# Where the one-hot rows of the mask come from: one load on ScalarE's queue and a copy on GpSimd, with clears and the identity moved between engines

## The chip, the cores and the metric

The kernel runs on one core of one Trainium2 chip. Its time is the device time of one execution in microseconds (us). A profiled execution gives, besides, a span from the first to the last instruction and the trace that is quoted below. The engines are TensorE (PE, its weight loads PEld), VectorE (DVE), ScalarE (ACT), GpSimd (POOL) and SyncE (SP); SPq, ACTq and POOLq are transfers issued from the queues of those engines.

## The reference

Block-sparse attention over 4 batches, 8 heads, 768 positions and 64 channels, and behind it a mixer over the positions and a two-layer network:

```python
# attention, block = 32, 24 blocks
scores = scale * (q @ k^T)
mask = |blk_i - blk_j| <= 1, or the first or last block on either side,
       or kb in sampled_blocks[qb]           # 3 sampled blocks per block of queries
attn = softmax(where(mask, scores, -1e9))
x = (attn @ v), heads side by side           # (4, 768, 512)
# mixer and network
u = x + (x^T @ U @ V)^T                      # U: 768x32, V: 32x768
out = u + max(u @ w_ch1, 0) @ w_ch2          # 512 -> 2048 -> 512
```

The inputs are float32 (`sampled_blocks` integers), the output is float32.

## The kernel before

Work goes by 16 pairs of heads, 4 for each batch. The head dimension of one head is 64, so a head's q or k, turned, fills 64 partitions. The four pairs of the first batch carry the mask in the score product itself: the other 64 partitions of the same tile hold, for q, the **one-hot rows** (24 rows by 768 columns, row z is 1 where the column's query lies in block z) and, for k, the **mask rows** (24 rows that hold 0 or -240 for each block of queries against each key). One product of 128 rows then gives score plus mask. The tiles are `qres[0]`, `qres[1]`, `kres[0]` and `kres[1]`, parts of one tile `res` of 128 x 4 x 2 x 768 halves. Head 0 has its data in partitions 0 to 63 and its mask rows from partition 64 on; head 1 has its data in 64 to 127 and its mask rows from partition 0 on (`mrows`). What lies beside the 24 rows must be zero. From batch 1 on, scores are plain and are multiplied by a 0/1 `mask` tile, which is made from the product of `kmask` (the mask rows, zero elsewhere) and the one-hot rows (`mask_part`, lines 944 to 955).

The opening block (lines 234 to 349) is written out by hand and each engine runs its instructions in the order written:

- Each queue's transfers. SP loads q and k of head 0, the one-hot rows of head 1 and then of head 0 (`one_hot`, line 187), q and k of head 1, then v of pair 0 and all of pair 1, `moe_U`, the second set (`second_set`: one-hot rows into `qres[1]`, mask rows copied from `kres[0]` into `kres[1]` and `kmask`), `moe_V`. ScalarE's queue loads `small` (identity in halves, block numbers, fixed mask) and `sb` (the sampled blocks).
- VectorE clears the mask halves of `qres[0]` and `kres[0]`, `bias` and `Ut`, and then makes `bias` (24 x 48, the mask by blocks) out of `sb` in three instructions (lines 311, 315, 318).
- ScalarE loads its table with a first exponential and makes `id32`, the identity in float32, out of `small` (line 307).
- TensorE runs seven products on a constant (`keep_warm`), turns head 0's q and k in float32 with `id32` (`first_turn`, line 226), and spreads `bias` over the columns with `mask_half` (line 279), whose operand is head 1's one-hot rows. `first_row` (line 297) and `mask_row` (line 287) bring the results out of PSUM into `qres[0]` and `kres[0]`.
- GpSimd clears `qres[1]` and `kres[1]`, sets the ones columns of `vt`, casts head 1's q and k (line 213), clears `Vt` and `kmask` (line 343), and then casts what each load brings (line 131).

Behind it a long `PLAN` string gives the order of everything else, a word for each step. Its first words are scores of head 0 (`S0 S3 e e S5 B0`: `S` one score block, line 987; `B` two, line 1006; `e` its exponential on ScalarE, lines 996 and 1014), then head 1's turns (`Z`, line 359), value products (`A`, line 421), the turns of pair 1 (`R`, line 960) and the mask products (`K`, line 946). Later stages are the other batches' scores (line 1037), the first layer (line 692) and the second (line 767).

Of the kernel before, what the change touches and what calls it, by code (L numbers as in the profile page):

```python
# [12 lines left out]
FP32 = mybir.dt.float32  # L13
# [6 lines left out]
P = 128  # L20
# [3 lines left out]
def kernel(  # L24
# [14 lines left out]
    nc = tc.nc  # L39

    B, H, S, D = q.shape
    BLK = 32
    NB = S // BLK
# [13 lines left out]
    ii = np.arange(NB)  # L57
# [6 lines left out]
    ).astype(np.float32)  # L64
    cols = np.arange(S)
    blk = ((cols % P) * T + cols // P) // BLK
    ohT_np = (blk[None, :] == ii[:, None]).astype(np.float16)
    small_np = np.zeros((P, NB + 1 + P // 2), np.float32)
    small_np[:NB, :NB] = (ms_np - 1.0) * -MASK_BIAS
    small_np[:NB, NB] = ii  # L70
# [3 lines left out]
    ohT_dr = nc.inline_tensor(ohT_np, name="one_hot_const")  # L74
# [14 lines left out]
    def bank(n, shape, dtype):  # L89
        ap = PS[:, n, :]  # L90
        if dtype != FP32:
            ap = ap.bitcast(dtype)
        ap = ap[:, 0 : int(np.prod(shape[1:]))]
        return ap.rearrange("p (a b) -> p a b", a=shape[1]) if len(shape) > 2 else ap
# [3 lines left out]
    def psc2():  # L98
        ring["psc"] += 1
        return PS[:, (0, 3)[ring["psc"] % 2] :][:, 0:2]  # L100
# [4 lines left out]
    id16 = small[:, NB + 1 :].bitcast(FP16)  # L105
# [5 lines left out]
    kmask = consts.tile([P, S], FP16, name="kmask")  # L111
    res = consts.tile([P, 4, 2, S], FP16, name="res")
    qres = [res[:, i] for i in range(2)]
    kres = [res[:, 2 + i] for i in range(2)]
    drows = [slice(0, D), slice(D, P)]
    mrows = [slice(D, D + NB), slice(0, NB)]
# [5 lines left out]
    Ut = wpool.tile([P, T, P], FP16)  # L122
    Vt = wpool.tile([P, T, P], FP16)
# [52 lines left out]
    def first_load(h, n, queue):  # L176

        src, nm = ((q, "qld"), (k, "kld"))[n]
        if h == 0:
            lds[nm] = ldpool.tile([P, 2, T, D], FP32, tag="ld" + nm, name=nm)  # L180
            sts[0, nm] = stpool.tile([P, T, 2, D], FP16, tag="st" + nm, name="st" + nm)
        queue.dma_start(
            out=lds[nm][:, h], in_=src[0, h].rearrange("(p t) d -> p t d", t=T)
        )

    def one_hot(i, h):
        nc.sync.dma_start(out=qres[i][mrows[h], h, :], in_=ohT_dr.ap())

    warm = nc.const_aps.tensor(1.0, [P, 512], mybir.dt.bfloat16)
    bias = consts.tile([P, 2, D], FP16)  # L190

    def second_set():
        for h in range(2):
            one_hot(1, h)
            nc.sync.dma_start(out=kres[1][mrows[h], h, :], in_=kres[0][mrows[h], h, :])
        nc.sync.dma_start(out=kmask[mrows[0], :], in_=kres[0][mrows[0], 0, :])

    def load_mix_u():
        uld = ldpool.tile([P, T, R], FP32, tag="ldu", name="uld", bufs=1)
        nc.sync.dma_start(out=uld, in_=moe_U.rearrange("(p t) r -> p t r", t=T))  # L200
        nc.gpsimd.tensor_copy(out=Ut[:, :, 0:R], in_=uld)
# [9 lines left out]
    def first_cast(h, n, copy):  # L211
        nm = ("qld", "kld")[n]
        copy(out=sts[0, nm][:, :, h], in_=lds[nm][:, h])
# [3 lines left out]
    id32 = consts.tile([P, P], FP32)  # L217

    def first_turn(n, c):

        nm = ("qld", "kld")[n]
        twos = ((0, 1, 2), ()) if n == 0 else ((0,), (1, 2))
        pt = pw[:, 1, 0:HS] if n == 0 else bank(5 + c, [P, HS], FP32)
        first_out[n, c] = pt
        for j, t in enumerate(twos[c]):
            nc.tensor.matmul(
                pt[:, j * P : (j + 1) * P],
                lds[nm][:, 0, 2 * t : 2 * t + 2].rearrange("p t d -> p (t d)"),
                id32,
                is_transpose=True,  # L230
                start=(j == 0), stop=(j == len(twos[c]) - 1), skip_group_check=True,
            )

    with tc.manual_schedule(
        engines={
            mybir.EngineType.PE,
            mybir.EngineType.DVE,
            mybir.EngineType.Activation,
            mybir.EngineType.SP,
            mybir.EngineType.Pool,  # L240
        }
    ):
        first_load(0, 0, nc.sync)
        first_load(0, 1, nc.sync)
        nc.scalar.dma_start(out=small, in_=small_dr.ap())
        nc.scalar.dma_start(
            out=sb[0:NB].rearrange("k z r w -> k (z r w)"),
            in_=sampled_blocks.bitcast(I32)
            .rearrange("z r -> (z r)")[None, :]
            .broadcast_to([NB, NB * 6]),  # L250
        )
        for h in (1, 0):
            nc.vector.memset(qres[0][(slice(D, P), slice(0, D))[h], h, :], 0.0)
            one_hot(0, h)
        nc.vector.memset(bias, 0.0)
        for h in range(2):
            nc.vector.memset(kres[0][(slice(D, P), slice(0, D))[h], h, :], 0.0)
        for n in range(2):
            first_load(1, n, nc.sync)
        for tile_ in (qres[1], kres[1]):  # L260
            nc.gpsimd.memset(tile_.bitcast(FP32), 0.0)
        for vt in vts:
            nc.gpsimd.memset(vt[:, :, :, D : D + 1], 1.0)
        first = consts.tile([P, 1], FP32)
        nc.scalar.activation(
            out=first, in_=nc.const_aps.tensor(1.0, [P, 1], FP32), func=AF.Exp
        )
        pw = psc2()

        def keep_warm(n, cols=512):  # L270
            for _ in range(n):
                nc.tensor.matmul(
                    pw[:, 0, 0:cols], warm[:, 0:P], warm[:, 0:cols], start=True, stop=True
                )

        pks = [bank(2, [P, HS], FP32), bank(7, [P, HS], FP32)]

        def mask_half(c):
            nc.tensor.matmul(
                pks[c],  # L280
                bias[0:NB].rearrange("k a z -> k (a z)"),
                qres[0][mrows[1], 1, c * HS : (c + 1) * HS],
                start=True, stop=True,
            )

        def mask_row(h, c, copy, lo=0, hi=HS):
            copy(
                out=kres[0][mrows[h], h, c * HS + lo : c * HS + hi],
                in_=pks[c][mrows[h], lo:hi],
            )  # L290

        def first_row(n, c, u, copy):
            t0, m = (0, 3) if n == 0 else ((0, 1), (1, 2))[c]
            dst = (qres, kres)[n][0][drows[0], 0, :].rearrange(
                "p (t u c) -> p t u c", u=2, c=P
            )
            copy(
                out=dst[:, t0 : t0 + m, u],
                in_=first_out[n, c][drows[u], 0 : m * P].rearrange(
                    "p (t c) -> p t c", c=P  # L300
                ),
            )

        neq = consts.tile([P, NB, 3], FP32)
        a01 = consts.tile([P, NB], FP32)
        nc.vector.memset(Ut, 0.0)
        nc.scalar.copy(out=id32, in_=id16)
        psc2()
        keep_warm(6)
        keep_warm(1, 256)  # L310
        nc.vector.tensor_tensor(
            out=neq[0:NB], in0=sb[0:NB, :, :, 0],
            in1=iota[:, :, None].broadcast_to([NB, NB, 3]), op=ALU.not_equal,
        )
        nc.vector.tensor_reduce(
            out=a01[0:NB], in_=neq[0:NB], axis=mybir.AxisListType.X, op=ALU.min
        )
        nc.vector.scalar_tensor_tensor(
            out=bias[0:NB, :, 0:NB], in0=a01[0:NB, None].broadcast_to([NB, 2, NB]),
            scalar=MASK_BIAS, in1=ms[:, None].broadcast_to([NB, 2, NB]),  # L320
            op0=ALU.mult, op1=ALU.max,
        )
        first_turn(0, 0)
        first_row(0, 0, 0, nc.scalar.copy)
        first_row(0, 0, 1, nc.scalar.copy)
        first_turn(1, 0)
        first_row(1, 0, 0, nc.vector.tensor_copy)
        mask_half(0)
        mask_row(0, 0, nc.vector.tensor_copy, 0, P)
        first_turn(1, 1)  # L330
        first_row(1, 0, 1, nc.vector.tensor_copy)
        mask_half(1)
        first_row(1, 1, 0, nc.scalar.copy)
        mask_row(0, 0, nc.vector.tensor_copy, P, HS)
        first_row(1, 1, 1, nc.vector.tensor_copy)
        mask_row(0, 1, nc.vector.tensor_copy)
        mask_row(1, 0, nc.vector.tensor_copy)
        mask_row(1, 1, nc.vector.tensor_copy)

        for n in range(2):  # L340
            first_cast(1, n, nc.gpsimd.tensor_copy)
        for tile_ in (Vt, kmask):
            nc.gpsimd.memset(tile_.bitcast(FP32), 0.0)
        load_v(0)
        load_qk(1)
        load_v(1)
        load_mix_u()
        second_set()
        load_mix_v()

# [840 lines left out]
```

## Time and profile before

| | |
|---|---|
| median of 3 runs | 270.18 us (269.74 to 270.96) |
| the profiled execution | 270.59 us |
| its span | 268.8 us |
| granted TensorE clock | 1.00 |
| busy: PE, DVE, ACT, POOL | 262.3, 232.5, 202.8, 72.6 us |

In rows of a timeline the columns are start and duration in us, engine, line of the kernel, operation, output<-input, shape and count; in brackets is how long the engine had stood idle before and what ended that. The chain that ended last is followed back from the last instruction, at each step to what released it. TensorE's products are pipelined and their ends are modelled, so that a shown product can run on under the next one.

### The profile page before, as it was taken

Reading aid. Unit: us, or ns where it says so; the run is one execution under the profiler, and the core shown is the slowest. Engines: PE = TensorE matmul, PEld = TensorE weight load, DVE = VectorE, ACT = ScalarE, POOL = GpSimd, SP = SyncE. Lnnn points to the kernel's source line nnn. Section 1 sums busy time; section 2 is a strip of 40 time slices with the busy share of each in tenths; the row PEclk is TensorE's granted clock in tenths of the full one; section 3 lists DMA queues with packets and bytes.
Section 4 is the critical chain, followed back from the end, with each engine's and each line's share of the span. In section 5 each row is a group of like instructions: output and inputs, shape, how many; then the busy total and the mean of one; then the engine's idle time right before and its main releaser. Section 6 shows DMA issues by size and latency. Waiting matters only on the chain.

```text
span 268.8 us, 7294 instructions
## 1 busy us (share of the span) xinstructions
PE 262.3 (98%) x2999; PEld 182.1 (68%) x2999; DVE 232.5 (86%) x477; ACT 202.8 (75%) x265; POOL 72.6 (27%) x98
## 2 busy tenths in 40 slices
PE   8899999999999999999999999999999999999995
PEld 3577776565667778665666887565667788666884
DVE  6589988988999998867588997688998999999993
ACT  5989998897989666788898857788997944789200
POOL 4558307199072470070706160000000000000000
PEclk9999999999999999999999999999999999999999
DMA  6787998999999999998928998620200115400024
GB/s 184 243 277 263 212 195 177 189 132 173 135 159 118 123 81 99 287 103 90 91 34 76 97 99 154 219 39 7 56 0 2 39 44 117 159 2 0 2 98 137
DMA packets 88720, 31.66 MB, mean 118 GB/s; under 512 B 77104, under 2 KB 85840, under 8 KB 88688
## 3 DMA queue, kind: packets, MB, share of 16 engines
q0 software_dynamic: 49728, 10.10, 46.7%
q1 hardware_dynamic: 38492, 20.86, 32.6%
q8 instruction: 23, 0.38, 0.6%
q10 hardware_dynamic: 468, 0.26, 0.4%
q14 instruction: 9, 0.07, 0.1%
HBM read 27.67 MB, written 6.29 MB: 126 GB/s over the span
## 4 chain that ended last, share of the span: by engine, by line
PE 78%; DMA 9%; DVE 6%; ACT 3%; SPq 1%; issue 1%; POOL 0%; DVEq 0%; ACTq 0%
PE ps L767 32%; PE ps L692 22%; PE ps L421 10%; PE ps L1037 9%; DMA kpl<-stkld 3%; DMA vld<-in_v_dram 3%; DMA qld<-in_q_dram 2%; PE ps L987 1%; DMA kmask<-res 1%; ACT est L1046 1%; PE ps L1006 1%; PE ps L672 1%; DVE est L1052 1%; DVE xf L558 1%; DVE res L976 1%
## 5 line engine op out<-in xcount | busy, mean ns | idle before, releaser
L1046 ACT ACTIVATE est<-ps 128x1536 f16<-128x1536 f32 x72 | 100.6, 1450 | 19.0 <-PE ps L1037 19.0
L692 PE MATMUL ps<-uT,w1t 128*128 128x384 f16 x384 | 70.3, 326 | 0.0
L1052 DVE TENSOR_TENSOR est<-est,mask 128x1440 f16<-128x1440 f16 x72 | 63.5, 902 | 0.7 <-ACT est L1046 0.2
L692 PEld LDWEIGHTS <-w1t 128*128 128x128 f16 x384 | 35.6, 97 | 26.6 <-issue 6.8
L421 PEld LDWEIGHTS <-est 128*128 128x128 f16 x1152 | 40.5, 97 | 6.8 <-issue 3.0
L421 PE MATMUL ps<-vt,est 128*128 128x65 f16 x1152 | 43.3, 193 | 0.1
L767 PEld LDWEIGHTS <-hid 128*128 128x128 f16 x358 | 34.0, 98 | 6.6 <-issue 1.6
L704 ACT ACTIVATE hid<-ps 128x384 f16<-128x384 f32 x63 | 29.7, 496 | 4.7 <-PE ps L692 4.3
L1037 PE MATMUL ps<-qpl,kpl 64*128 64x512 f16 (+1 forms) x288 | 31.7, 325 | 0.2 <-DMA kpl<-stkld 0.2
L767 PE MATMUL ps<-w2t,hid 128*128 128x256 f16 x238 | 31.1, 273 | 0.0
L139 POOL DMA_DIRECT2D stqld<-in_q_dram x20 | 16.3, 820 | 54.2 <-DMA qpl<-stqld 53.9
L886 DVE TENSOR_TENSOR xf<-xf,ps 128x256 f32<-128x256 f32 x63 | 25.3, 414 | 4.1 <-PE ps L767 3.7
L706 DVE TENSOR_SCALAR hid<-ps 128x384 f16<-128x384 f32 x33 | 18.3, 554 | 8.8 <-PE ps L692 8.0
L767 PEld LDWEIGHTS <-sums 128*128 128x128 f16 x216 | 20.1, 98 | 4.4 <-issue 1.0
L996 ACT ACTIVATE est<-ps 128x768 f16<-128x768 f32 x30 | 22.5, 812 | 0.4 <-PE ps L987 0.3
L1037 PEld LDWEIGHTS <-kpl 64*128 64x128 f16 x288 | 12.3, 94 | 14.5 <-issue 9.1
L767 PE MATMUL ps<-res,sums 128*128 128x256 f16 x144 | 19.4, 273 | 0.0
L139 POOL DMA_DIRECT2D stkld<-in_k_dram x20 | 16.3, 819 | 8.9 <-DMA kpl<-stkld 8.0
L641 ACT CAST xh<-xf 128x384 f16<-128x384 f32 x24 | 11.0, 510 | 10.0 <-DVE xf L637 10.0
L558 DVE TENSOR_TENSOR xf<-ps,rcp 128x384 f32<-128x384 f32 x32 | 17.7, 553 | 0.8
L139 POOL DMA_DIRECT2D vt<-in_v_dram x20 | 16.3, 820 | 0.0
L767 PE MATMUL ps<-res,hid 128*128 128x256 f16 x120 | 15.9, 273 | 0.0
(119 smaller groups left out, 338.6 us busy)
## 6 DMA issues: line engine op xcount, KB each, us to landing
out_dram<-xf SPq DMA_DIRECT2D x18, 256.0 KB, 2.4
vld<-in_v_dram SPq DMA_DIRECT2D x6, 384.0 KB, 6.7
w1t<-in_moe_w_ch_dram POOLq DMA_DIRECT2D x4, 512.0 KB, 8.2
w2t<-in_moe_w_ch_dram POOLq DMA_DIRECT2D x4, 512.0 KB, 8.3
qld<-in_q_dram SPq DMA_DIRECT2D x5, 384.0 KB, 3.9
kld<-in_k_dram SPq DMA_DIRECT2D x5, 384.0 KB
stqld<-in_q_dram POOLq DMA_DIRECT2D x20, 96.0 KB, 3.7
stkld<-in_k_dram POOLq DMA_DIRECT2D x20, 96.0 KB, 4.3
```

The costliest lines, as they stand in the source:

```text
L139: nc.gpsimd.dma_start(out=dst[:, h], in_=src[b, 2 * hp + h].rearrange("(p t) d -> p t d", t=T),)
L421: nc.tensor.matmul(pav[:, sc, :], est[:, n, sc * P : (sc + 1) * P], vts[b % 2][:, 2 * hp + h, g, 0 : D + 1], start=(g == 0 and sc == 0), s ...
L558: nc.vector.tensor_tensor(out=dst, in0=pav[:, :, 0:D], in1=rcp[:, :, None].broadcast_to([P, T, D]), op=ALU.mult,)
L692: nc.tensor.matmul(pt, w1t[:, cc, jj * P : (jj + 1) * P], bts[b].uT[:, cc, c * HS : (c + 1) * HS], start=(cc == 0), stop=(cc == NCC - 1), ...
L704: nc.scalar.activation(out=dst, in_=pt, func=AF.Relu)
L706: nc.vector.tensor_scalar_max(out=dst, in0=pt, scalar1=0.0)
L767: nc.tensor.matmul(acc[key], lhsT, rhs, start=(first and i == 0), stop=(i == len(pairs_) - 1), skip_group_check=True,)
L886: nc.vector.tensor_add(out=x, in0=x, in1=acc[a, b, tau])
L996: lambda: nc.scalar.activation(out=dst, in_=ps, func=AF.Exp, scale=0.125),
L1037: nc.tensor.matmul(units[h][:, u * S + lo : u * S + hi], kT[drows[h], g * P : (g + 1) * P], qT[drows[h], lo:hi], start=True, stop=True, sk ...
L1046: nc.scalar.activation(out=both[h], in_=units[h].rearrange("p (g n) -> p g n", g=2), func=AF.Exp, scale=0.125,)
L1052: lambda: nc.vector.tensor_mul(out=masked(both[h]), in0=masked(both[h]), in1=masked(mask[:, 2 * j : 2 * j + 2, :]),),
```

## The change

Seven edits, all in the opening block and the helpers that it calls:

- The one-hot constant has 32 rows in place of 24; the last eight are zero.
- It is loaded once for the first pair, for head 1, as the second transfer of ScalarE's queue, ahead of `sb`. The two loads on SP go.
- GpSimd copies those 32 rows in SBUF to head 0's place, behind its clears.
- VectorE's clears of `qres[0]` take the 32 partitions that the one-hot rows don't fill, and so nothing has to wait for them before the load.
- `Ut` is cleared by GpSimd in place of VectorE, and `kmask` before the copy in place of behind the casts of head 1.
- `id32` is made by VectorE in place of ScalarE, at the place where `Ut` was cleared. One more `keep_warm` product of 256 columns stands before the first `mask_half`.
- In the second set the copy of the mask rows into `kmask` comes second of five in place of last, and the two one-hot loads come before the two other copies.

```diff
-    ohT_np = (blk[None, :] == ii[:, None]).astype(np.float16)
+    ohT_np = (blk[None, :] == np.arange(32)[:, None]).astype(np.float16)
...
     def one_hot(i, h):
-        nc.sync.dma_start(out=qres[i][mrows[h], h, :], in_=ohT_dr.ap())
+        nc.sync.dma_start(out=qres[i][mrows[h], h, :], in_=ohT_dr.ap()[0:NB, :])
...
     def second_set():
+        one_hot(1, 0)
+        nc.sync.dma_start(out=kmask[mrows[0], :], in_=kres[0][mrows[0], 0, :])
+        one_hot(1, 1)
         for h in range(2):
-            one_hot(1, h)
             nc.sync.dma_start(out=kres[1][mrows[h], h, :], in_=kres[0][mrows[h], h, :])
-        nc.sync.dma_start(out=kmask[mrows[0], :], in_=kres[0][mrows[0], 0, :])
...
         nc.scalar.dma_start(out=small, in_=small_dr.ap())
+        nc.scalar.dma_start(out=qres[0][0:32, 1, :], in_=ohT_dr.ap())
         nc.scalar.dma_start(
             out=sb[0:NB].rearrange("k z r w -> k (z r w)"),
...
         for h in (1, 0):
-            nc.vector.memset(qres[0][(slice(D, P), slice(0, D))[h], h, :], 0.0)
-            one_hot(0, h)
+            nc.vector.memset(qres[0][(slice(D + 32, P), slice(32, D))[h], h, :], 0.0)
         nc.vector.memset(bias, 0.0)
...
         for vt in vts:
             nc.gpsimd.memset(vt[:, :, :, D : D + 1], 1.0)
+        for tile_ in (Ut, kmask):
+            nc.gpsimd.memset(tile_.bitcast(FP32), 0.0)
+        nc.gpsimd.tensor_copy(out=qres[0][D : D + 32, 0, :], in_=qres[0][0:32, 1, :])
...
-        nc.vector.memset(Ut, 0.0)
-        nc.scalar.copy(out=id32, in_=id16)
+        nc.vector.tensor_copy(out=id32, in_=id16)
...
         first_row(1, 0, 0, nc.vector.tensor_copy)
+        keep_warm(1, 256)
         mask_half(0)
...
-        for tile_ in (Vt, kmask):
-            nc.gpsimd.memset(tile_.bitcast(FP32), 0.0)
+        nc.gpsimd.memset(Vt.bitcast(FP32), 0.0)
```

## The prediction

> **What bounds the kernel now.** I read the page first, then the chain that ended last over the first 54 us, then the timeline of the head in two windows, ScalarE's timeline behind it, and the transfers of the first 8 us.
>
> ```profile
> span 268.8 us, 7294 instructions
> ...
> PE 262.3 (98%) x2999; PEld 182.1 (68%) x2999; DVE 232.5 (86%) x477; ACT 202.8 (75%) x265; POOL 72.6 (27%) x98
> ```
>
> TensorE is called busy for 262.3 of 268.8 us, so all idle time is worth 6.5 us at most. The diff touches only the head, and the chain (start, duration, what) says what the head waits for:
>
> ```profile
> 2.50 0.36 SPq L182
> ...
> 3.85 6.40 DMA qld<-in_q_dram
> ...
> 10.31 3.85 DMA kmask<-res
> ...
> 44.51 8.23 DMA kpl<-stkld
> ...
> 52.79 0.82 PE ps L1037 x8
> ```
>
> A load of q issued at 3.85 on SyncE's queue (SP) lands at 10.25 and lets SP issue the copy into `kmask`, which lands at 14.16. Behind that the chain goes over compute engines, and two more transfers, to 52.79, from where it is TensorE to the end. The two loads of pair 1 also stop TensorE directly (timeline, 8 to 15 us; the bracket is idle time before the row and what ended it):
>
> ```profile
> 10.30 0.83 POOL L131 CAST stqld<-qld 128x768 f16<-128x768 f32 x1 [1.02 <-DMA qld<-in_q_dram]
> 10.31 0.72 SPq L196 DMA_DIRECT2D kmask<-res  x1
> 10.90 1.45 ACT L1014 ACTIVATE est<-ps 128x1536 f16<-128x1536 f32 x1 [0.20 <-PE ps L1006]
> ...
> 11.18 0.51 PE L960 MATMUL ps<-small,stqld 128*128 128x128 f16 x6 [0.32 <-POOL stqld L131]
> ...
> 11.72 0.83 POOL L131 CAST stkld<-kld 128x768 f16<-128x768 f32 x1 [0.60 <-DMA kld<-in_k_dram]
> ...
> 12.25 0.81 ACT L996 ACTIVATE est<-ps 128x768 f16<-128x768 f32 x1
> ...
> 12.61 0.51 PE L960 MATMUL ps<-small,stkld 128*128 128x128 f16 x6 [0.41 <-POOL stkld L131]
> ...
> 13.06 0.83 POOL L131 CAST vt<-vld 128x768 f16<-128x768 f32 x1 [0.51 <-DMA vld<-in_v_dram]
> 13.07 0.40 SPq L153 DMA_DIRECT2D qld<-in_q_dram  x1
> ...
> 13.14 0.81 PE L1006 MATMUL ps<-res 128*128 128x512 f16 x4
> ...
> 13.99 1.45 ACT L1014 ACTIVATE est<-ps 128x1536 f16<-128x1536 f32 x1 [0.93 <-PE ps L1006]
> 14.21 0.10 PEld L946 LDWEIGHTS <-kmask 128*128 128x128 f16 x1 [0.20 <-DMA kmask<-res]
> ...
> 14.46 1.56 POOL L207 CAST Vt<-vld 32x768 f16<-32x768 f32 x1 [0.28 <-DMA vld<-in_moe_V_dram]
> ```
>
> The turns of pair 1 (L960) wait 0.32 and 0.41 us for GpSimd's casts, which wait for the loads; the double score block behind them starts at 13.14, and ScalarE, which has had work without a pause of more than 0.20 since 10.90, stands for 0.93. After that no load stops ScalarE for long:
>
> ```profile
> 22.50 7.24 ACT L996 ACTIVATE est<-ps 128x768 f16<-128x768 f32 x10
> ```
>
> Ten exponentials end to end: the order is one of full engines there, so a shift at 14 us should pass through. Two pairs of rows also show how SP is held: its issues at 10.31 and 13.07 begin within 0.01 us of casts whose loads have just landed. By the list of SP's transfers those loads are eight issues earlier, so I take eight SP transfers as the limit in flight.
>
> **The change part by part.** The start of the head:
>
> ```profile
> 0.73 0.37 ACTq L245 DMA_DIRECT2D small<-small_const  x1
> ...
> 0.78 2.93 PE L272 MATMUL ps<-const-bfloat16-1.0 128*128 128x512 bf16 x7 [0.78 <-PEq L1175]
> ...
> 1.13 0.69 ACTq L246 DMA_DIRECT2D sb<-in_sampled_blocks_dram  x1
> ...
> 1.65 0.80 SPq L187 DMA_DIRECT2D res<-one_hot_const  x2
> ...
> 2.08 0.52 POOL L263 MEMSET vt<- 128x48 f16 x2
> ...
> 2.98 0.38 DVE L306 MEMSET Ut<- 128x384 uint32 x1
> ...
> 3.26 0.28 ACT L307 CAST id<-small 128x128 f32<-128x128 f16 x1
> ...
> 3.59 0.90 PE L226 MATMUL ps<-id,qld 128*128 128x128 f32 x3
> 3.60 0.22 DVE L311 TENSOR_TENSOR neq<-sb,small 24x72 f32<-24x72 int32 x1 [0.24 <-DMA sb<-in_sampled_blocks_dram]
> ...
> 4.11 0.20 DVE L318 SCALAR_TENSOR_TENSOR bias<-a,small 24x48 f16<-24x48 f32 x1
> ...
> 4.53 1.42 ACT L297 CAST res<-ps 64x384 f16<-64x384 f32 x3 [0.99 <-PE ps L226]
> 4.63 0.09 PEld L279 LDWEIGHTS <-bias 24*128 24x128 f16 x1 [0.32 <-DVE bias L318]
> ...
> 4.86 0.32 PE L279 MATMUL ps<-res,bias 24*128 24x384 f16 x1 [0.16 <-DMA res<-one_hot_const]
> ...
> 5.21 0.29 DVE L287 CAST res<-ps 24x128 f16<-24x128 f32 x1 [0.19 <-PE ps L279]
> ...
> 5.74 1.40 PE L987 MATMUL ps<-res 128*128 128x384 f16 x6
> ...
> 6.28 1.51 ACT L996 ACTIVATE est<-ps 128x768 f16<-128x768 f32 x2 [0.33 <-PE ps L987]
> ...
> 6.75 1.13 DVE L287 CAST res<-ps 24x384 f16<-24x384 f32 x2
> ...
> 7.08 0.42 POOL L343 MEMSET kmask<- 128x384 f32 x1
> ```
>
> *SP's two one-hot issues go.* The next load, of head 1's q, moves from 2.50 to 1.65: every later load is issued 0.85 us earlier. Whether it lands as much earlier depends on the transfer engines. This is the rate by 0.2 us over the first 8 us:
>
> ```profile
> GB/s 0 0 0 0 0 0 0 0 21 80 137 265 332 385 360 399 330 169 46 100 115 254 315 330 346 300 253 254 300 253 277 253 215 154 154 123 230 261 200 230
> ```
>
> It falls from 330 to 169, 46, 100, 115 and 254 between 3.4 and 4.4 us: against 330 that is 161+284+230+215+76 = 966, times 0.2 us 193 KB, or 0.59 us of transfers not made, because the loads came late behind the one-hots. Loads issued 0.85 earlier fill this hole. One one-hot of 32 rows by 768 halves (48 KB) in place of two of 24 (72 KB) is 24 KB less, 0.07 us at that rate. Together 0.66; the ends are 0.07 (engines full, only bytes count) and 0.85 (issue alone counts). I take 0.66, since the hole is in the row. [...]
>
> *What earlier loads do.* The q cast moves from 10.30 to 9.64 and the first turn needn't wait its 0.32: 10.86. The k cast moves from 11.72 to 11.06, ends at 11.89; the second turn, at 12.61 less 0.41 less 0.32 = 11.88, is held to about 11.94. The double block follows 0.53 later as now (13.14 less 12.61), at 12.47; its banks are free, since the exponential that reads them ends at 10.90+1.45 = 12.35. Its own exponential begins 0.85 after it, as now: 13.32 in place of 13.99. **Gain 0.67.** What is late next is ScalarE itself, free at 12.25+0.81 = 13.06, so 0.26 of the pause stays.
>
> *The mask rows' copy moves up* in SP's list and becomes the eighth after head 1's q, long landed by then. It now waits for VectorE's row at 6.75, which ends at about 7.3, and is issued near 7.35 in place of 10.31; behind it on SP stand only the second set's rows and the loads of pair 2, which wait for v's landing anyway. It runs behind v of pair 1 (13.06 less 0.66 = 12.40); now it lands 1.10 after v with three small copies ahead, so 12.4 to 13.5, and I take 12.9, for one copy ahead. The mask products need it at 14.21 less 0.20 less 0.67 = 13.34: hidden, by 0.4, and at the upper end 0.16 late.
>
> *ScalarE's queue.* The one-hot costs one more issue, about 0.40 (0.80 for two), ahead of `sb`. Its landing goes from 3.60 to 4.00, and `bias`, which ends 0.71 after that landing, from 4.31 to 4.71. The mask product (L279) began at 4.86: its weights came 0.32 after `bias`, and 0.16 went on the one-hot. The one-hot's wait goes; the later `bias` takes its place. With 0.05 to 0.39 from `bias` to the product it begins between 4.76 and 5.10; I take 4.96. So the mask row, the first score (5.74) and the first exponential (6.28) come 0.10 **later**, with ends of -0.10 and +0.25. ScalarE's table load moves 0.4 later, with nothing on its path: it waited 0.99 before 4.53.
>
> *Identity on VectorE.* It takes the place of the clear of `Ut` at 2.98, and has 0.20 to 0.28 to run (0.28 on ScalarE at 3.26); the first turns can begin at about 3.25 rather than 3.59. That 0.3 is covered by the mask, which is later; without that cover it is a gain of up to 0.3. The extra 256-column filler is half of 2.93/7, 0.21, in TensorE's wait ahead of the mask product: nothing, or 0.05 if the identity is no earlier.
>
> *GpSimd.* Its clears end at 2.60 and get two more of 0.42: about 3.4. The narrower clears on VectorE have the same columns and cost the same. Then it copies 32x768 for head 0, on which the first score waits. The one-hot is issued at 1.13; `sb`, issued there now, took 2.4 us to land, the mask copy 3.85: 3.55 to 4.98, and I take 3.9, near `sb`, which has the same queue and hour. The copy has no row; the cast of 128x768 took 0.83, the strided one of 32 rows 1.56; I take 0.83 for its plain rows. Done at 4.73, 1.0 before it is needed. At the worst ends, 6.54, the first score is 0.80 late. [...]
>
> Sum: 0.67 less 0.10, about 0.6 us. On the profiled execution (270.59, span 268.8) that gives 270.0 and a span of 268.2; against the median of the runs, 270.18, it gives **269.6**, or -0.2%. A measurement of this kernel can tell about 0.5%, 1.35 us, from no change, so my forecast is a small gain inside that.
>
> **The rivals.** *The start moves up as well.* If `sb` lands no later, the product can go at 4.70, where it waited only for the one-hot, and with the turns 0.3 earlier the first score may gain 0.15 to 0.3; with 0.67 to 0.72 behind it, 1.0 us: **269.2**. For it: three waits at the start go. Against it: an issue of 0.4 stands before `sb`.
>
> *Hidden anyway.* The engines are near their rate from 4.4 us on, and the loads land only 0.07 earlier. The pause of 0.93 stays, and the start's 0.10 is taken up in it: **270.1**. Against it is the hole at 3.4 to 4.4.
>
> *Slower: GpSimd's copy holds the first score.* From one-hot landing plus copy of 5.74+0.67 = 6.41 on, the delay eats the gain. At 6.54 it gives +0.1; with a landing like that of the 3.85 row, 6.40 after issue (7.53), and 0.83, the score starts at 8.4, 2.65 late, less 0.67: +2.0, **272.2**. GpSimd's casts of head 1 queue behind it. Against it: the one-hot is 48 KB, and not behind those loads.
>
> **How the numbers follow.** Forecast 0.50, start also 0.18, hidden 0.18, copy 0.14. The forecast's own range is 269.1 to 270.1 (start -0.10 to +0.25, late mask copy 0.16, loads 0.07 to 0.85). The range of all, 268.7 to 271.0, leaves out some of the first rival's best end and most of the third. Three runs of one kernel lie 1.2 us apart, so the forecast can be read as faster by over 0.5% at 0.10 of its 0.50, the first rival at 0.10 of 0.18; the third gives slower at 0.10 and the rest of both 0.03. Faster 0.20, same 0.67, slower 0.13.
>
> **What would show it.** Right: SP's load of head 1's q at about 1.65; the casts of pair 1 near 9.6 and 11.1; the double block's pause on ScalarE 0.2 to 0.3 in place of 0.93; `kmask` issued near 7.4 and no wait on it; `neq` near 4.0 on `sb`; the first score near 5.8 with VectorE as its releaser; TensorE's row behind 52.79 earlier by 0.6. Wrong: the first score waiting for GpSimd; casts of pair 1 where they were; a chain past 20 us that doesn't shift by the same amount.

## The result, and the profile after

The changed kernel takes 271.72 us (median of 9 runs, 270.65 to 272.77) against 270.23 (9 runs, 269.74 to 271.05): a ratio of 1.0048, 95% interval 1.003 to 1.0067. It is slower by 0.5%, where 0.2% faster was forecast, and outside the range. (The ratio compares the runs themselves and is not the quotient of the two medians.) The profiled execution took 271.72 us with a span of 269.9, 1.1 more than before. Three lines of the page of the changed kernel: the span, the engines' busy time, and the shares of the chain that ended last.

```profile
span 269.9 us, 7295 instructions
...
PE 262.8 (97%) x3000; PEld 182.5 (68%) x3000; DVE 232.3 (86%) x477; ACT 202.7 (75%) x264; POOL 73.8 (27%) x100
...
PE 87%; DVE 6%; ACT 4%; DMA 1%; issue 1%; ACTq 0%; DVEq 0%
```

Transfers were 9% of the chain and are 1%, about all of it the load of `sb`. In kmask_early, below, which has the one-hot loads of before, they are 1% too, and in sb_first and sp_held, which keep most of the change, 7 and 6%. So this share isn't put down to the change. What makes the head late stands in the timeline of the first 7.5 us (start, duration, engine, line, operation; idle time before it and its releaser):

```profile
1.13 0.45 ACTq L247 DMA_DIRECT2D res<-one_hot_const  x1
...
1.61 0.68 ACTq L248 DMA_DIRECT2D sb<-in_sampled_blocks_dram  x1
1.65 0.43 SPq L182 DMA_DIRECT2D qld<-in_q_dram  x1
...
3.16 0.23 DVE L310 CAST id<-small 128x128 f32<-128x128 f16 x1 [0.24 <-DMA small<-small_const]
...
3.53 0.52 PE L227 MATMUL ps<-id,qld 128*128 128x128 f32 x3
...
3.81 0.82 POOL L267 COPY res<-res 32x768 f16<-32x768 f16 x1 [0.54 <-DMA res<-one_hot_const]
...
4.30 0.27 PE L276 MATMUL ps<-const-bfloat16-1.0 128*128 128x256 bf16 x1
...
5.24 0.22 DVE L314 TENSOR_TENSOR neq<-sb,small 24x72 f32<-24x72 int32 x1 [1.85 <-DMA sb<-in_sampled_blocks_dram]
...
6.00 0.33 PE L283 MATMUL ps<-res,bias 24*128 24x384 f16 x1 [1.42 <-DVE bias L321]
```

`sb`, issued 0.48 later than before, lands 1.64 later (5.24 against 3.60), and TensorE stands idle for 1.42 us. The next view, TensorE's timeline of the head, and four windows of 0.25 us over all engines (in each row the third number from the end is the granted clock) show the second cost:

```profile
6.89 2.09 PE L990 MATMUL ps<-res 128*128 128x384 f16 x6
8.77 1.49 PE L1009 MATMUL ps<-res 128*128 128x512 f16 x4
```

```profile
6.75:7.00 0.25, 0.25 (x2) 0.11 (x2) 0.24 (x2) 0.25 (x1) 0.25 (x2) 0.89 1.11 356
7.00:7.25 0.25, 0.25 (x2) 0.00 (x1) 0.25 (x1) 0.10 (x1) 0.25 (x1) 0.50 0.94 350
10.00:10.25 0.25, 0.25 (x3) 0.20 (x2) 0.00 (x0) 0.00 (x0) 0.12 (x1) 0.50 0.75 206
10.25:10.50 0.25, 0.25 (x7) 0.25 (x5) 0.00 (x0) 0.21 (x1) 0.25 (x1) 0.78 0.17 37
```

A mean of 0.89 over 0.25 us is 0.055 us at a clock of 0.50, and one of 0.78 is 0.11 us. So the granted clock is 0.50 from about 6.95 to 10.36, for some 3.4 us by this estimate, and six score products take 2.09 in place of 1.40. TensorE had stood idle for 1.42 us, up to 6.00, and the clock was still 1.00 from there to about 6.95. Then part of the loss comes back (timeline from 7.4 us, and ScalarE's from 13):

```profile
7.73 2.21 ACT L999 ACTIVATE est<-ps 128x768 f16<-128x768 f32 x3 [0.64 <-PE ps L990]
...
8.85 0.83 POOL L131 CAST stqld<-qld 128x768 f16<-128x768 f32 x1 [0.16 <-DMA qld<-in_q_dram]
...
10.12 0.83 POOL L131 CAST stkld<-kld 128x768 f16<-128x768 f32 x1 [0.45 <-DMA kld<-in_k_dram]
...
12.97 1.45 ACT L1017 ACTIVATE est<-ps 128x1536 f16<-128x1536 f32 x1 [0.20 <-PE ps L1009]
```

```profile
15.31 1.45 ACT L1017 ACTIVATE est<-ps 128x1536 f16<-128x1536 f32 x1 [0.20 <-PE ps L1009]
...
23.83 7.24 ACT L999 ACTIVATE est<-ps 128x768 f16<-128x768 f32 x10
```

Read against the rows of before: the first exponential 7.73 for 6.28 (+1.45), the second double block's 12.97 for 10.90 (+2.07, behind products at a clock of 0.50), the third's 15.31 for 13.99 (+1.32: the pause of 0.93 is gone), the ten exponentials 23.83 for 22.50 (+1.33). At the end of the span 1.1 of it is left: the profile of the kernel before waits for `kpl` at 52.79, and this one doesn't.

### The profile page after: what moved, and what is told of

It is laid out like the page before. It is cut to its first block, busy times and chain, and to the rows that moved or that the text cites. A ratio compares the mean times of both kernels' runs of the same rounds, so it can differ in the third digit from the quotient of the medians.

```text
span 269.9 us, 7295 instructions
## 1 busy us (share of the span) xinstructions
PE 262.8 (97%) x3000; PEld 182.5 (68%) x3000; DVE 232.3 (86%) x477; ACT 202.7 (75%) x264; POOL 73.8 (27%) x100
## 3 DMA queue, kind: packets, MB, share of 16 engines
HBM read 27.64 MB, written 6.29 MB: 126 GB/s over the span
## 4 chain that ended last, share of the span: by engine, by line
PE 87%; DVE 6%; ACT 4%; DMA 1%; issue 1%; ACTq 0%; DVEq 0%
PE ps L770 32%; PE ps L695 23%; PE ps L424 11%; PE ps L1040 10%; PE ps L990 3%; PE ps L1009 3%; ACT est L1017 2%; ACT est L1049 1%; DMA sb<-in_sampled_blocks_dram 1%; PE ps L675 1%; DVE est L1055 1%; DVE xf L561 1%; ACT hid L707 1%; PE ps L949 1%; PE ps L963 1%
```

## The experiments

Theory: the head is late because one small transfer lands late, and TensorE's idle time behind it costs clock on top. Rivals: another edit costs by itself; the early SP loads or GpSimd's copy do.

All profiles of the head side by side. "Ten" is the start of the ten exponentials, and six is the duration of the six score products (1.26 to 1.40 in eight profiles, 2.09 or 2.10 in nine).

| kernel | `sb` issued | `neq` starts | six | ten | span | median, ratio (interval) |
|---|---|---|---|---|---|---|
| before | 1.13 | 3.60 | 1.40 | 22.50 | 268.8 | 270.23 |
| before_again | 1.13 | 3.75 | 1.40 | 22.57 | 270.0 | one run |
| kmask_early | 1.13 | 4.00 | 1.26 | 21.68 | 267.8 | 270.33, 1.0005 (0.9979 to 1.0032) |
| rest_only | 1.13 | 3.67 | 2.10 | 23.54 | 269.9 | 270.60, 1.0006 (0.9985 to 1.0027) |
| less_warm | 1.14 | 3.79 | 2.10 | 23.57 | 269.6 | 271.33, 1.0042 (1.0021 to 1.0062) |
| sb_first | 1.13 | 3.83 | 1.32 | 22.62 | 268.7 | 272.07, 1.0064 (1.004 to 1.0088) |
| sb_first_warm | 1.13 | 3.87 | 1.32 | 23.11 | 269.2 | 271.01, 1.0017 (0.9999 to 1.0036) |
| oh_on_sp | 1.14 | 3.87 | 2.10 | 23.63 | 270.2 | 271.52, 1.0034 (1.0014 to 1.0055) |
| oh_on_sp_warm | 1.13 | 3.69 | 1.32 | 23.18 | 269.4 | 270.68, 1.0015 (0.9996 to 1.0034) |
| oh_on_pool | 1.13 | 3.61 | 2.10 | 24.96 | 271.1 | 271.70, 1.0044 (1.0021 to 1.0066) |
| after | 1.61 | 5.24 | 2.09 | 23.83 | 269.9 | 271.72, 1.0048 (1.003 to 1.0067) |
| warm_filler | 1.61 | 4.61 | 1.40 | 23.21 | 269.4 | 271.12, 1.0034 (1.0019 to 1.0049) |
| sp_held | 1.61 | 4.89 | 2.10 | 23.73 | 269.9 | 271.75, 1.005 (1.003 to 1.0069) |
| before_plus_load | 1.61 | 4.83 | 1.40 | 22.50 | 268.8 | 272.21, 1.0077 (1.0055 to 1.0099) |
| small_load | 1.61 | 5.00 | 2.10 | 23.51 | 270.1 | 271.94, 1.0051 (1.0029 to 1.0073) |
| sp_pause | 1.61 | 4.45 | 2.10 | 23.58 | 270.0 | one run |
| k_late | 1.61 | 4.00 | 2.10 | 25.62 | 271.7 | one run |

The kernel before ran beside each group; its median was 270.06 to 270.67. A profile is one execution. In sb_first and before_plus_load it is the fastest of all their runs, in rest_only and oh_on_pool the slowest, so the medians speak for the kernels and the profiles for what can happen in one.

### What delays the transfer

**sb_first**: `sb` ahead of the one-hot.

```diff
+        nc.scalar.dma_start(out=sb[0:NB]..., in_=sampled_blocks...)
         nc.scalar.dma_start(out=qres[0][0:32, 1, :], in_=ohT_dr.ap())
-        nc.scalar.dma_start(out=sb[0:NB]..., in_=sampled_blocks...)
```

> The changed kernel with one swap: on ScalarE's queue sb goes ahead of the one-hot rows. Theory 1 (sb's landing is the whole loss; it is late because of what stands ahead of it or runs beside it): neq starts near 3.6 us as in the kernel before, in place of 5.24; TensorE is not idle for more than 0.5 us ahead of the mask product, its granted clock stays 1.00 in 6 to 10 us in place of 0.50; the first exponential is at 6.2 to 6.4 in place of 7.73, and with the loads of pair 1 earlier the tenth column of ScalarE's row at 13.99 comes near 13.3: 269.5 us, some 0.6 below the kernel before. Theory 2 (the earlier stream of SP's loads makes sb late wherever it stands): neq still at 4.5 or later, time 271 to 271.7. A new wait could be the one-hot itself: GpSimd's copy then starts near 4.3 to 5 and must end by 5.7.

`neq` came back to 3.83, so SP's early loads do not hold up an `sb` that is issued at 1.13; but the time did not come back (269.5 was expected, the median is 272.07). Its timeline shows the wait handed on to the other transfer:

```profile
1.85 0.31 ACTq L253 DMA_DIRECT2D res<-one_hot_const  x1
...
3.83 0.22 DVE L314 TENSOR_TENSOR neq<-sb,small 24x72 f32<-24x72 int32 x1 [0.28 <-DMA sb<-in_sampled_blocks_dram]
...
5.71 0.32 PE L283 MATMUL ps<-res,bias 24*128 24x384 f16 x1 [0.89 <-DMA res<-one_hot_const]
...
5.81 0.82 POOL L267 COPY res<-res 32x768 f16<-32x768 f16 x1 [2.53 <-DMA res<-one_hot_const]
```

The one-hot, issued third, at 1.85, lands 3.86 us after that. In either order the third transfer of ScalarE's queue is the late one; whether its place there or the later issue makes it so, the next runs show.

**before_plus_load**, **small_load**: the kernel before with a load of 48 KB, or 6 KB, between `small` and `sb`.

```diff
+        nc.scalar.dma_start(out=hid[0:32, ...], in_=ohT_dr.ap())            # before_plus_load
+        nc.scalar.dma_start(out=hid[0:32, 0, 0, 0:96], in_=ohT_dr.ap()[:, 0:96])  # small_load
         nc.scalar.dma_start(out=sb[0:NB]..., in_=sampled_blocks...)
```

> The kernel before with one load more: the one-hot constant of 32 rows is loaded on ScalarE's queue between small and sb, into a tile that nothing reads yet. SP's queue is as before, with its pause behind the two one-hot loads. Theory 1a (sb waits behind those 48 KB on ScalarE's own queue): neq near 5.2 or at least 4.8, a clock of 0.50 for some 3 us, 271.5 to 272 us. Theory 1b (sb waits because SP's loads of head 1 come without a pause): only the issue counts, neq near 4.1, about 0.5 later than before, clock 1.00, 270.4 to 270.9 us.

> The kernel before with a load of 6 KB (32 rows of 96 halves) between small and sb on ScalarE's queue, where before_plus_load had 48 KB. If sb is late by the bytes ahead of it, neq comes near 4.1 (0.48 for the issue), in place of 4.83, and the time is 270.3 to 270.9. If it is late because it is issued 0.48 later, into engines that SP's loads have filled by then, neq is at 4.6 or later, and the half clock shows in most runs: 271.3 to 272.3.

`neq` at 4.83 and 5.00 (one row of each timeline):

```profile
4.83 0.22 DVE L314 TENSOR_TENSOR neq<-sb,small 24x72 f32<-24x72 int32 x1 [1.46 <-DMA sb<-in_sampled_blocks_dram]
```

```profile
5.00 0.22 DVE L312 TENSOR_TENSOR neq<-sb,small 24x72 f32<-24x72 int32 x1 [1.64 <-DMA sb<-in_sampled_blocks_dram]
```

Eight times fewer bytes ahead made `neq` no earlier (5.00 behind 6 KB, 4.83 behind 48 KB): what counts here is the later issue, 1.61 for 1.13, not the bytes of its own queue. And this one load, alone, costs the kernel before at least as much as the whole change. Not all of that is `sb`: the identity is made on ScalarE here, behind the longer queue, at 3.73 in place of 3.26, and TensorE waits 0.35 for it in both profiles.

**sp_held** (SP's pause put back), **sp_pause** (SP issues nothing between 1.6 and 3.6), **k_late** (head 0's k held back too):

```diff
+        nc.sync.dma_start(out=hid[0:NB, ...], in_=ohT_dr.ap()[0:NB, :])   # sp_held: twice, ahead of head 1's loads
...
+        nc.vector.memset(lds["qld"][:, 1, 0, 0:1], 0.0)   # sp_pause: behind id32, for q and k; head 1's loads wait for it
+        nc.vector.memset(lds["kld"][:, 0, 0, 0:1], 0.0)   # k_late: head 0's k load as well
```

> The changed kernel with SP's pause put back: two loads of 24 one-hot rows into a tile that nothing reads yet stand ahead of the loads of head 1. Theory 1a (sb waits behind the one-hot on ScalarE's queue): neq stays at 5.0 to 5.2 and the time at 271.7 or above, since the loads of pair 1 lose their gain. Theory 1b (SP's stream without a pause): neq comes to about 4.1, the clock stays 1.00, 270.2 to 270.8 us.

> The changed kernel, in which SP's loads of head 1 wait for a clear by VectorE that stands behind the identity, so that SP issues nothing from about 1.6 to 3.4 us; the transfers on ScalarE's queue are as in the changed kernel. Its own time is not the question (the loads come late). If sb is late because SP's stream behind the first two loads fills the engines, neq comes to 4.0 to 4.2 (issue 0.48 later, landing 2.4 to 2.5 after it). If the two loads of head 0 that are already in flight are enough, it stays at 4.6 to 5.2.

> sp_pause with head 0's k load held back by a VectorE clear as well, so that only head 0's q load is in flight on SP when sb is issued at 1.61. If the loads of head 0 are what sb stands behind, neq comes to 4.0 to 4.2 here and not in sp_pause. If it is still at 4.6 or later, SP's loads aren't the reason, and it is the place behind another transfer on ScalarE's queue.

`neq` at 4.89 with the pause filled by small loads, 4.45 with SP silent, and 4.00 with only one load of SP in flight. The first two lie between the values that were expected; the third is as expected:

```profile
4.89 0.22 DVE L319 TENSOR_TENSOR neq<-sb,small 24x72 f32<-24x72 int32 x1 [1.31 <-DMA sb<-in_sampled_blocks_dram]
```

```profile
4.45 0.49 DVE L316 TENSOR_TENSOR neq<-sb,small 24x72 f32<-24x72 int32 x1 [0.86 <-DMA sb<-in_sampled_blocks_dram]
```

```profile
3.94 0.82 POOL L266 COPY res<-res 32x768 f16<-32x768 f16 x1 [0.65 <-DMA res<-one_hot_const]
...
4.00 0.83 DVE L319 TENSOR_TENSOR neq<-sb,small 24x72 f32<-24x72 int32 x1 [0.39 <-DMA sb<-in_sampled_blocks_dram]
```

By these runs SP's loads are the reason (`neq` at 5.24 in the changed kernel, at 4.45 and 4.00 with them held back), not the place in ScalarE's queue, which is the same in all three. Counted from its issue, `sb` lands after 2.5 to 2.9 us in the ten profiles in which it is issued at 1.13 or 1.14, after 3.0 to 3.6 in the five in which it is issued at 1.61 and SP goes on loading, and after 2.4 and 2.8 in k_late and sp_pause. The three groups rest on single executions (the same `sb` landed at 4.61 in warm_filler and at 5.24 in the changed kernel), so what each load of SP adds stays open.

**oh_on_sp**, **oh_on_pool**: the one load on SP, third, or first on GpSimd's queue.

```diff
-        nc.scalar.dma_start(out=qres[0][0:32, 1, :], in_=ohT_dr.ap())
+        nc.sync.dma_start(out=qres[0][0:32, 1, :], in_=ohT_dr.ap())     # oh_on_pool: nc.gpsimd, as the first load
```

> The changed kernel with its one-hot load moved from ScalarE's queue to SP's, third there, where the first of the two stood before; everything else of the change stays. Theory 1 (whatever is third on ScalarE's queue lands 3.6 to 3.9 us after its issue, in place of 2.4, and TensorE's idle time behind it brings the half clock): neq is back near 3.6, the one-hot lands near 4.8 as in the kernel before, GpSimd's copy runs from about 4.85 to 5.67, the first score is near 5.75, the clock stays 1.00, and the loads of pair 1 keep 0.4 of their 0.85: 269.5 to 270.0 us. Theory 2 (the rest of the change costs something by itself, such as the copy or the identity on VectorE): neq near 3.6 and still 270.8 or more.

> The changed kernel with its one-hot load as the first thing on GpSimd's queue, ahead of the clears. Theory 1: sb is second on ScalarE's queue again and neq near 3.6; the one-hot, issued near 0.8 to 1.5, lands at 3.5 to 4.5; GpSimd's clears come 0.8 later, its copy at 4.3 to 5.2; the first score at 5.6 to 5.8, clock 1.00, loads of pair 1 0.85 earlier: 269.3 to 269.9 us. Against it: three queues then share the engines, and sb may still be late (neq at 4.5 or more, 271 us and above).

Both missed. On SP `neq` is at 3.87, but the one-hot lands near 5.3, later than the 4.8 of before, and the six score products take 2.10 in the profile (in oh_on_sp_warm, below, it lands at 6.27). On GpSimd's queue it landed near 6.1, and there VectorE's identity is late as well (last section). None of the versions with one load beats the kernel before.

### What the idle time costs

**warm_filler**, and the same for the two kernels above (**sb_first_warm** four products, **oh_on_sp_warm** two):

```diff
         keep_warm(1, 256)
+        keep_warm(6)
         mask_half(0)
```

> The changed kernel with six more constant products of 512 columns (about 1.3 us) ahead of the first mask product, so that TensorE has work while it waits for bias. sb and neq should stay near 5.2. Theory 1 with a clock part: the granted clock stays 1.00 in 6 to 10 us, the double score block at 8.77 takes about 0.9 in place of 1.49, the first exponential comes near 7.4 in place of 7.73 and the one of the first double block near 9.6 in place of 10.29: 0.5 to 0.7 us come back, 271.0 to 271.2. If the clock costs nothing at the end (the loads of pair 1 or ScalarE hold the order anyway), the time stays at 271.7.

> sb_first with four more constant products of 512 columns ahead of the first mask product, for the time in which TensorE waits for the one-hot. By the theory (a late transfer in the head, and the half clock behind TensorE's idle time) the group of runs at 271.5 to 272.7 goes; what is left is the one-hot's landing near 5.7, against which the earlier loads of pair 1 work: the ten exponentials begin near 22.6 as in the fastest run of sb_first, 270.3 to 270.8 us, all runs within 1 us. If the group stays, the clock is not its reason.

> oh_on_sp with two more constant products of 512 columns ahead of the first mask product, in the time for which TensorE waited for the one-hot there. If oh_on_sp's two groups of times (270.1 to 270.9 and 271.4 to 272.0) are two states of the clock, the upper group goes and the runs lie within 0.8 us of each other, at 270.3 to 270.8. If not, both groups stay.

```profile
7.19 1.40 PE L991 MATMUL ps<-res 128*128 128x384 f16 x6
```

With the filler warm_filler's six products take 1.40, its 12 runs lie within 1.1 us, and the median is 271.12, as expected: 0.6 below the changed kernel's, though the two intervals overlap. In its profile `bias` is ready at 5.52 and the products of the filler hold the mask product until 6.29, so a shorter one might give back more; that wasn't run. sb_first shows the effect most plainly: the ratio goes from 1.0064 to 1.0017, and its runs at 271.5 to 272.7 are gone (270.8 to 271.4, where 270.3 to 270.8 was expected). In oh_on_sp it goes from 1.0034 to 1.0015, again with overlapping intervals, and one run of oh_on_sp_warm is still at 271.87.

**less_warm**: the kernel before, two fillers fewer at the start.

```diff
-        keep_warm(6)
+        keep_warm(4)
```

> The kernel before with two of its seven constant products at the start left out (four of 512 columns and one of 256 remain), so that TensorE stands still for some 0.9 us ahead of the first turn. No transfer and no other engine changes, and the first turn waits for the identity until 3.54 anyway. If idle time of TensorE in the head costs by the clock, the six score products at about 5.74 take 2.1 us in place of 1.40 in most executions and the time is 270.9 to 272. If the clock doesn't depend on it, the time stays at 270.2.

```profile
3.67 0.89 PE L226 MATMUL ps<-id,qld 128*128 128x128 f32 x3 [0.82 <-ACT id L307]
...
6.21 2.10 PE L987 MATMUL ps<-res 128*128 128x384 f16 x6
```

No transfer is issued at another time (`neq` 3.79), and 0.82 us of idle TensorE alone cost 0.42%. The six products are the witness: in this profile, as in seven others of the table, they take 2.10 and the granted clock does not show it. Its mean over the execution is 0.998 to 1.000 in these eight (0.993 in the changed kernel's), and in oh_on_sp, oh_on_pool, small_load and sp_held it is 1.00 in both windows from 6 to 10 us. In these eight the three turns on q already take 0.87 to 0.90, and the products behind are slow too. Only in the changed kernel's profile are the turns fast (three in 0.52) and the six products slow behind them (2.09, at a clock of 0.50). Nor does the idle time of one execution decide: rest_only, below, has 2.10 with no pause of TensorE over 0.23 ahead of them, while sb_first's profile has 1.32 behind one of 0.89. What is shown is that idle time moves the median of many runs; how much of it is too much is not.

### The other edits

**rest_only**: both one-hot loads on SP again, of 32 rows, no copy; all else of the change kept. **kmask_early**: the kernel before with the second set's new order alone. **before_again**: no edit.

```diff
-        nc.scalar.dma_start(out=qres[0][0:32, 1, :], in_=ohT_dr.ap())
+        nc.sync.dma_start(out=qres[0][0:32, 1, :], in_=ohT_dr.ap())
+        nc.sync.dma_start(out=qres[0][D : D + 32, 0, :], in_=ohT_dr.ap())
-        nc.gpsimd.tensor_copy(out=qres[0][D : D + 32, 0, :], in_=qres[0][0:32, 1, :])
```

> The changed kernel with its one-hot part undone: both one-hot rows come by two loads on SP, third and fourth, as in the kernel before, and GpSimd copies nothing; the moved clears, the identity on VectorE, the filler and the second set's order stay. If the transfers are the cause, this is the kernel before again within its noise: neq near 3.6 to 4.0, the mask product near 4.8, first exponential near 6.3, 270.0 to 270.5 us. If one of the other edits costs by itself, it stays at 270.9 or more.

> The kernel before with one part of the change alone: the second set's order, with the copy into kmask second. By the prediction's reading its landing moves from 14.16 to about 12.5 to 13.5, the wait of 0.20 on it goes, and since the loads of pair 1 still hold the turns, the time stays within 0.2 us of the kernel before: 270.0 to 270.3. If kmask's landing was what the chain hung on, 0.2 or more is gained. It also shows a second time where the head's loads land in the kernel before: the casts of pair 1 near 10.3, 11.7 and 13.1, if that was no accident of one execution.

> The kernel before once more, for a second profile of it. If the loads' landing in the first profile (casts of pair 1 at 10.30, 11.72 and 13.06) was one execution's, they come at other times here, such as kmask_early's 9.72, 10.73 and 12.19, with the same issues on SP; the pause of 0.93 on ScalarE's row is then smaller or gone, and the gain of 0.67 that the prediction took from it was not to be had in most executions.

The moved clears, the identity, the filler and the order of the second set make no measurable difference together (1.0006, and 0.27% at the upper end of the interval), nor does the order alone (1.0005). rest_only's interval lies below the changed kernel's, so the loss is in the one-hot part. Its profile, the slowest of its 12 runs, is not the kernel before again: the six products take 2.10.

```profile
3.64 0.87 PE L227 MATMUL ps<-id,qld 128*128 128x128 f32 x3
...
5.17 0.47 PE L283 MATMUL ps<-res,bias 24*128 24x384 f16 x1 [0.23 <-DMA res<-one_hot_const]
...
6.62 2.10 PE L990 MATMUL ps<-res 128*128 128x384 f16 x6
```

before_again has the pause on ScalarE at the same place, so it was no accident of one profile. But both profiles of the kernel before are slower than the median of the runs beside them (270.59 against 270.23, and 271.77 against 270.06), and kmask_early's, at 269.60, has no such pause, with pair 1 loaded as before (casts at 9.72 and 10.73). First before_again, then kmask_early:

```profile
14.05 1.45 ACT L1014 ACTIVATE est<-ps 128x1536 f16<-128x1536 f32 x1 [0.94 <-PE ps L1006]
```

```profile
13.17 1.45 ACT L1015 ACTIVATE est<-ps 128x1536 f16<-128x1536 f32 x1 [0.20 <-PE ps L1007]
```

In kmask_early the ten exponentials begin 0.82 earlier than in the first profile. So in how many executions of the kernel before the pause was there to be gained stays open. before_again's span is 1.2 longer than the first profile's, and its chain of 36 to 56 us says where: the transpose that lands at 52.75 in the first profile lands at 53.85 here, behind a v load of 8.11 us in place of 7.01.

```profile
36.68 8.11 DMA vld<-in_v_dram
...
45.79 8.05 DMA kpl<-stkld
...
53.90 0.82 PE ps L1037 x8
```

## Why the prediction was wrong

The step that failed is *ScalarE's queue*. It gave `sb` the delay of its issue, 0.40, and so took the landing to come as long after the issue as before (2.47). The landing was 1.64 later, 3.63 after the issue. The row of before is of a transfer issued at 1.13, when SP's loads had hardly begun; issued 0.48 later it runs beside them, and k_late, where `sb` lands at 4.00, has the forecast delay with these loads held back. The prediction's own rows held a sign of this: the mask product of before waits until 4.86 for a one-hot that is issued from 1.65 on, 3.2 earlier. And it filled the hole in SP's stream itself, but priced `sb` as if nothing there had changed.

A second term was missing: slow products behind the idle time (in the changed kernel's profile a granted clock of 0.50 for some 3.4 us, and 2.09 for six products in place of 1.40). The prediction counted TensorE's wait ahead of the mask product only as a wait. less_warm prices 0.82 us of idle time at 0.42% by itself, and the changed kernel's was 1.42; filling it gave back 0.6 of the 1.5 us (warm_filler).

The rival that had the sign right, GpSimd's copy holding the first score, was wrong in its mechanism: the copy runs at 3.81 to 4.63, as forecast (3.9 to 4.73), and the first score waits for VectorE's mask row. But the copy has a cost that the prediction gave it nothing for: had `sb` landed at 4.00, `neq` would have met it: in k_late `neq` takes 0.83 in place of 0.22 and ends 0.07 after the copy.

Right were: SP's load at 1.65; the cost of VectorE's narrower clears (two of 32x384 take 0.87, where two of 64x384 took 0.89); the casts of pair 1 earlier (8.85 and 10.12, where 9.64 and 11.06 were forecast); no wait on `kmask`, though it is issued only at 8.52, when the mask rows are done, and not at 7.35; VectorE as the first score's releaser; and that a shift at 14 us passes through: from the start of the ten exponentials to the end of the span it is 246.0 to 246.6 us in every profile above but before_again's (247.4).

The gain of 0.67 looks right and isn't shown. The pause of 0.93 is down to 0.20, worth 0.75, but it is 0.20 in all fifteen profiles other than the two of the kernel before, also where pair 1 is loaded no earlier: in rest_only the casts come at 10.70 and 12.11, and the late first score alone hides the loads. Nor is the size of the shift, 0.66, borne out: the eight profiles with SP's loads as before have the q cast anywhere from 9.03 to 10.70, the five with loads 0.85 earlier from 8.72 to 9.21. The turns' 0.3 wasn't there either: the identity on VectorE waits for `small` to land and starts at 3.16, and the first turn at 3.53 in place of 3.59.

Beside the gain, the sum failed in one term, +0.10 at the first exponential, which measured +1.45 and, with the clock at 0.50, +2.07 at the second double block's.

## What to carry to other kernels

In this head a short transfer that the critical chain waits for is priced by what is in flight when it is issued (`sb` issued at 1.61 came at 4.00 with one load of SP in flight and at 4.61 to 5.24 with SP loading), not by the bytes ahead of it in its own queue (5.00 behind 6 KB, 4.83 behind 48 KB): the one that decides goes first, ahead of the bulk loads. Where TensorE's start hangs on such a transfer, fill its wait, since the idle time costs again: 0.82 us of it cost 0.42% in less_warm, and filling it took sb_first's ratio from 1.0064 to 1.0017. To see whether it did, time products of a known shape, since the granted clock can stand at 1.00 while they are slow (oh_on_sp's six took 2.10 at 6.79, with 1.00 in the windows from 6 to 10 us). Compare medians of many runs, because one profile can be the luckiest of ten. And read a gain off more than one profile of the kernel before.

## What the runs showed of the hardware

Two of VectorE's instructions took longer while GpSimd's ran. `neq` took 0.83, 0.49 and 0.42 us in k_late, sp_pause and warm_filler, where GpSimd's copy was running, and ended 0.07 to 0.08 after it each time; it takes 0.22 in the others, but for oh_on_pool. There the identity's cast met a series of clears:

```profile
3.21 1.33 DVE L310 CAST id<-small 128x128 f32<-128x128 f16 x1 [0.30 <-DMA small<-small_const]
3.24 0.54 POOL L264 MEMSET vt<- 128x48 f16 x2
3.38 0.71 POOL L266 MEMSET Ut<- 128x384 f32 x1
3.61 0.93 DVE L314 TENSOR_TENSOR neq<-sb,small 24x72 f32<-24x72 int32 x1
4.02 0.44 POOL L266 MEMSET kmask<- 128x384 f32 x1
```

The cast takes 0.23 in sb_first, where the clears are done before it; here it ends at 4.54, 0.08 behind the last of them, and `neq` with it. The time of TensorE's first products differs from one execution to the next: the three turns take 0.90 and 0.56 us in the two profiles of the kernel before, from 3.59 and 3.67 on, 0.64 in kmask_early (3.83) and 0.52 in the changed kernel (3.53).
